# An attention, Fourier-mixing and feed-forward kernel: every engine in a hand-timed order, value sums by accumulating DMAs, and a two-round start of the feed-forward part

## The chip, the cores and the metric

The kernel runs on one core of a Trainium2 chip. The core has five engines that take instructions in order from queues of their own and meet through semaphores: PE (matmul, with its weight loads shown apart as PEld), DVE (vector), ACT (scalar and activation), POOL (GpSimd) and SP (only issues DMAs here). [...] The metric is the device time of one execution in microseconds; of several runs the median is taken.

## The reference

Inputs are q, k, v of shape (8 batches, 8 heads, 576 positions, 64) and two weights w_ch1 (512 x 2048) and w_ch2 (2048 x 512), which arrive as float64. Attention is computed twice and added: on means over four neighbouring positions (repeated back), and in a band of plus or minus three positions.

```python
q_d = q.reshape(B, H, Sd, 4, D).mean(axis=3)     # k_d and v_d alike
out_up = np.repeat(sm_attn(q_d, k_d, v_d), 4, axis=2)
mask = np.abs(pos[:, None] - pos[None, :]) < 4
...
x = out_up + np.matmul(softmax(where(mask, scores, -1e9)), v)
# moe part, x as (batch, 576, 512)
mixed = np.real(fft(fft(x, axis=1), axis=2))
u = x + mixed
un = (u - mean(u)) / np.sqrt(var(u) + 1e-06)
out = u + np.maximum(un @ w_ch1, 0.0) @ w_ch2
```

## The kernel before

The work falls into a front (attention and Fourier mixing, batch by batch) and a feed-forward part.

Local attention goes in 40 units, five to a batch; a unit holds two windows of 64 positions for all heads. A unit loads a slice of q and k (tile qkT) and of v (vaug), adds fours of columns of qkT for the pooled attention (`sum_in`), multiplies scores (tile sc), takes maxima, exponentials (sb), transposes (tpl, pT) and multiplies by v (av); DVE divides and writes to the x tiles of the batch, xa and xb.

Pooled attention goes in four steps of two heads for a batch (sp, sd, tp, ptd, avd). Its values are sums of four rows of v: `sum_v` loads a tile raw by SP (L213) and POOL adds twice (L214, L215) into the tile vsum. The result odt is stored to a DRAM buffer ud by SP (L292, `store`), repeated four times on the way, and `add_up` (L451) has four DMAs issued by POOL that add ud onto xa and xb.

Mixing (`Mix`) then works with xs = xa + xb on DVE (L458) and xm = xa - xb on POOL (L459), folds them over channels (xeo, then again into xa), splits the folded values into a rounded part fh and a remainder fl (`split`, fl on POOL at L494), and multiplies by cosine matrices over the sequence (tile y, `sequence`, nine matmuls for each of four parts) and over the channels (tile mix). `unfold` forms the sum oa and the difference xm on POOL (L558), which SP stores to a DRAM buffer um.

The feed-forward part works on 36 tiles of 128 rows. Blocks of 5, 4, ..., 4, 3 tiles go through 16 chunks of 128 hidden columns. A chunk of a block, called an item here, is twelve matmuls into hps (`first`, L730: high and low weight parts times high and low inputs), a ReLU on ACT into hh, the remainder hl on DVE (L734), and three matmuls a tile into the accumulators acc (`second`, L746 to L748). Tiles are prepared for the next block beside it: load from um, statistics, `norm`, transposition (tpn).

The weights arrive as 64 quarters of 256 columns, as float64 words. `to_f32` joins the two words of each to float32 on DVE (L123, L126, L131), with an absolute value on ACT (L130) and a guard that zeroes tiny values, on POOL (L135, L136) or DVE (L138) by a pattern. `part_weights` writes the rounded part by ACT and the remainder by POOL (L161).

What sets the order: PE's queue holds the order in which the code calls matmuls (a hand-written loop over steps, with `Stream` objects that put in pieces of folding and mixing at due times). The queues of the other engines are filled by a scheduler from priorities and a simulated timeline. Feed-forward work starts when the loop over steps is done; with two of 16 weight chunks decoded ahead, the rest are decoded while block 0 runs.

```python
main = unit_step(s) if s < NU + LAG else [lambda: None] * 4
...
fold_stream.run(4 * s + i + 1)
product_stream.run(4 * s + i + 1)
```

Of the kernel before, what the change touches and what calls it, by code (L numbers as in the profile page):

```python
# [41 lines left out]
CHUNKS = (1, 3, 4)

AHEAD = 2
NUM_PLACES = 4

GUARDS = "cc-c-"
WARM_UP = 12

TINY_HIGH = 1.125 * 2.0**-15  # L50


@with_exitstack
def kernel(
# [29 lines left out]
    NBLK = len(SIZES)  # L84
# [23 lines left out]
    places = [(res.tile([P, DM], F32, name="raw0"), res.tile([P, HN], I32, name="wt0"))]  # L108
# [8 lines left out]
    turns = [0]  # L117

    def to_f32(words, t):

        lo, hi = words[:, :, 0], words[:, :, 1]
        turns[0] += 1
        nc.vector.tensor_scalar(  # L123
            out=t, in0=hi, scalar1=3, scalar2=0x3FFFFFFF, op0=ALU.logical_shift_left, op1=ALU.bitwise_and
        )
        nc.vector.scalar_tensor_tensor(  # L126
            out=t, in0=lo, scalar=29, in1=t, op0=ALU.logical_shift_right, op1=ALU.bitwise_or
        )
        m, x = lo.bitcast(F32), t.bitcast(F32)
        nc.scalar.activation(out=m, in_=hi.bitcast(F32), func=AF.Abs)  # L130
        nc.vector.scalar_tensor_tensor(  # L131
            out=t, in0=hi, scalar=-0x40000000, in1=t, op0=ALU.bitwise_and, op1=ALU.bitwise_or
        )
        if GUARDS[turns[0] % len(GUARDS)] == "c":
            nc.gpsimd.tensor_scalar(out=m, in0=m, scalar1=TINY_HIGH, scalar2=None, op0=ALU.is_ge)  # L135
            nc.gpsimd.tensor_mul(out=x, in0=m, in1=x)  # L136
        else:
            nc.vector.scalar_tensor_tensor(out=x, in0=m, scalar=TINY_HIGH, in1=x, op0=ALU.is_ge, op1=ALU.mult)  # L138
        return x

    def fetch(raw, tm, f, w, j):

        src = wq[w - 1, f, j]
        if wide:
            nc.sync.dma_start(out=raw.bitcast(I32), in_=src.bitcast(I32))
            raw = raw.bitcast(I32).rearrange("p (n two) -> p n two", two=2)
        else:
            raw = raw[:, 0:HN]
            nc.sync.dma_start(out=raw, in_=src)
        return to_f32(raw, tm) if wide else raw  # L150

    def part_weights(f, w, j, raw, tm):

        x = fetch(raw, tm, f, w, j)
        if w == 1:
            x = x.rearrange("p (c f) -> p c f", c=2)
            h, l = (t[:, 2 * j : 2 * j + 2, :] for t in wts[f, 1])
        else:
            h, l = (t[:, j * HN : (j + 1) * HN] for t in wts[f, 2])
        nc.scalar.copy(out=h, in_=x)  # L160
        nc.gpsimd.tensor_sub(out=l, in0=x, in1=h.bitcast(F32))  # L161

    HD = DM // 2
    TB = BLK // P

    plocal, p1, pmix, pxs = (ExitStack() for _ in range(4))
    pf = pmix.enter_context(tc.tile_pool(name="pf", bufs=1, side="right"))
    p2 = plocal.enter_context(tc.tile_pool(name="p2", bufs=2))
# [5 lines left out]
    px = pxs.enter_context(tc.tile_pool(name="px", bufs=1, side="right"))  # L174
    vsum = [pd.tile([GH, 2, H, D + 1], F32, name=f"vsum{i}") for i in range(2)]
    for t in vsum:
        nc.gpsimd.memset(t, 1.0)
    zeros = pd.tile([8, DM], F32, name="zeros")
# [4 lines left out]

    def bank(name, rows=P):
        return banks.tile([P, DM], F32, name=name, tag="ps")[:rows]

    last, before = (B - 1) % NUM_X, (B - 3) % NUM_X

    xab = [None] * NUM_X
    for i in ((last + 1 + k) % NUM_X for k in range(NUM_X)):  # L190
        pool = pf if i == last else res if i == before else px
        xab[i] = [pool.tile([P, NSL, DM], F32, name=f"x{i}{j}") for j in "ab"]
# [3 lines left out]
    def zero_rows(b):  # L196

        for lo, hi in ((HS + 1, NUD + 1), (NUD + HS + 1, 2 * NUD)):
            nc.sync.dma_start(out=ud[b][lo:hi, :], in_=zeros[: hi - lo])
# [4 lines left out]
    class Pooled:  # L204
        def __init__(self, b):
            self.b, self.vs = b, vsum[b % 2]
            self.sd, self.pts = {}, {}

        def sum_v(self, i):

            h0, t = 4 * (i // 2), i % 2
            raw = pd.tile([GH, 4, 4 * D], F32, name="raw", bufs=NUM_RAW)
            nc.sync.dma_start(out=raw.rearrange("g r c -> g (r c)"), in_=vg[self.b, i])  # L213
            nc.gpsimd.tensor_add(out=raw[:, 0:2], in0=raw[:, 0:2], in1=raw[:, 2:4])  # L214
            nc.gpsimd.tensor_add(  # L215
                out=self.vs[:, t, h0 : h0 + 4, 0:D],
                in0=raw[:, 0].rearrange("g (h d) -> g h d", d=D),
                in1=raw[:, 1].rearrange("g (h d) -> g h d", d=D),
            )

        def scores(self, h0):
            qT, kT = sums[self.b]
            sd = self.sd[h0] = pd.tile([GH, 4, G], F32, name="sd", bufs=1)
            sps = [bank("sp", GH)[:, : 2 * G].rearrange("p (a g) -> p a g", a=2) for _ in range(2)]
            for t in range(2):
                for hl, sp in enumerate(sps):
                    r = slice(hl * D, hl * D + D)
                    nc.tensor.matmul(
                        sp[:, t, :],
                        qT[r, h0 // 2, t * GH : (t + 1) * GH],  # L230
                        kT[r, h0 // 2, :],
                        start=True,
                        stop=True,
                    )
            for hl, sp in enumerate(sps):
                mx = pd.tile([GH, 2], F32, name="mxd", bufs=4)
                nc.vector.tensor_reduce(out=mx, in_=sp, axis=AX.X, op=ALU.max)
                nc.vector.tensor_scalar_mul(out=mx, in0=mx, scalar1=-(2.0**-7))
                for t in range(2):
                    nc.scalar.activation(  # L240
                        out=sd[:, 2 * hl + t, :],
                        in_=sp[:, t, :],
                        func=AF.Exp,
                        scale=2.0**-7,
                        bias=mx[:, t : t + 1],
                    )

        def transpose_p(self, h0):
            self.pts[h0] = []
            for hl in range(2):  # L250
                tp = bank("tp", GH)[:, : 2 * G].rearrange("p (a g) -> p a g", a=2)
                for kt in range(2):
                    for t in range(2):
# [4 lines left out]
                        )  # L258
# [754 lines left out]
```

## Time and profile before

| | us |
|---|---|
| runs | 1397.17, 2261.53, 1392.53 |
| median | 1397.17 |
| the profiled execution | 1391.41 |
| its span, first to last instruction | 1389.6 |

Busy times in the span: PE 1214.0 us, DVE 636.9, POOL 369.0, ACT 292.3. In the prediction's rows a window is written start:end in us from the span's start; PEclk is the granted share of TensorE's clock, and the DMA share is the mean busy share of the core's 16 DMA engines. In a group's row stand the line, the engine, the operation, output<-inputs, shapes, count, busy us, mean ns of one, and the idle time before them with what ended it.

The 40 slices of the page below are 34.7 us each; digits are tenths of the slice.

```profile
PE   6774687759568966988999999999999999999998
DVE  5765485847657678789711311313113122131111
POOL 5424243534533467788400000000000000000000
PEclk8585769678687678999999999999999999999999
```

The first fifteen slices are the front, slices 16 to 20 the joint with feed-forward block 0 and the decoding, and the rest is feed-forward alone.

### The profile page before, as it was taken

The page shows a single profiled execution, that of the slowest core. Times are in us where ns is not written, and L with a number is a line of the kernel's source. Part 1 is how long each engine was busy: PE and PEld are TensorE (multiplying, and loading weights), DVE is VectorE, ACT ScalarE, POOL GpSimd, SP SyncE. Part 2 cuts the span into 40 slices and gives each one's busy share as a digit, 9 for nine tenths or more (in the row PEclk, how much of TensorE's full clock was granted, in tenths as well). Part 3 has the DMA queues.
Part 4 walks back from the last instruction along what each step waited for, and adds up shares of the span by engine and source line. Part 5 has one row for each costly group of instructions (what it writes and reads, how often), then busy time and mean ns, then how long its engine had stood idle before and what let it go on. Part 6 is the DMA issues. An engine that isn't in the chain of part 4 may idle for free.

```text
span 1389.6 us, 20511 instructions
## 1 busy us (share of the span) xinstructions
PE 1214.0 (87%) x8236; PEld 998.6 (72%) x8236; DVE 636.9 (46%) x1428; ACT 292.3 (21%) x678; POOL 369.0 (27%) x388
## 2 busy tenths in 40 slices
PE   6774687759568966988999999999999999999998
PEld 4663565548457755877788888888888888888897
DVE  5765485847657678789711311313113122131111
ACT  2331222223223221344311111111111111111110
POOL 5424243534533467788400000000000000000000
PEclk8585769678687678999999999999999999999999
DMA  7754627355562543343200100101001010010000
GB/s 234 238 174 111 158 86 179 109 140 171 133 152 70 152 116 84 119 129 123 91 0 0 61 1 0 61 0 61 1 0 61 0 53 9 0 53 0 1 31 23
DMA packets 50496, 110.84 MB, mean 80 GB/s; under 512 B 5494, under 2 KB 5784, under 8 KB 50144
## 3 DMA queue, kind: packets, MB, share of 16 engines
q1 hardware_dynamic: 44128, 95.82, 22.4%
q0 software_dynamic: 6272, 13.70, 5.1%
q8 instruction: 65, 1.06, 0.3%
q14 instruction: 31, 0.25, 0.1%
HBM read 81.20 MB, written 28.46 MB: 79 GB/s over the span
## 4 chain that ended last, share of the span: by engine, by line
PE 64%; DMA 15%; DVE 11%; POOL 5%; issue 4%; ACT 1%; SPq 0%; DVEq 0%; POOLq 0%; ACTq 0%
PE hps L730 25%; PE acc L748 9%; PE acc L747 9%; PE acc L746 8%; DMA ud<-odt 4%; DMA qkT<-in_qk_dram 3%; DMA x1b<-ud 3%; PE mix L534 2%; PE y L507 2%; PE avd L270 2%; PE sc L346 2%; DMA x2b<-ud 2%; DMA x0b<-ud 2%; DVE wt L126 1%; DVE xeo L467 1%
## 5 line engine op out<-in xcount | busy, mean ns | idle before, releaser
L730 PE MATMUL hps<-unT,w1h 128*128 128x512 f32 (+2 forms) x1280 | 322.6, 374 | 20.6 <-DVE hl L734 10.8
L734 DVE SCALAR_TENSOR_TENSOR hl<-hps,hh 128x512 fp32r<-128x512 f32 (+2 forms) x160 | 101.6, 635 | 446.7 <-ACT hh L733 446.6
L730 PEld LDWEIGHTS hps<-unT,w1h 128*128 128x128 f32 x1280 | 234.1, 191 | 62.6 <-DVE hl L734 11.2
L748 PE MATMUL acc<-w2h,hl 128*128 128x512 f32 x576 | 229.5, 398 | 5.8 <-DVE hl L734 5.4
L746 PE MATMUL acc<-w2h,hh 128*128 128x512 f32 x576 | 230.5, 400 | 4.6 <-ACT hh L733 4.6
L747 PE MATMUL acc<-w2l,hh 128*128 128x512 f32 x576 | 229.1, 398 | 0.0
L733 ACT ACTIVATE hh<-hps 128x512 fp32r<-128x512 f32 (+2 forms) x160 | 88.8, 555 | 598.5 <-PE hps L730 598.5
L683 POOL TENSOR_TENSOR rstd<-rstd,mhalf 128x1 f32<-128x1 f32 x36 | 20.2, 607 | 555.2 <-DVE rstd L682 553.3
L730 PE MATMUL hps<-unT,w1l 128*128 128x512 f32 (+2 forms) x640 | 160.2, 372 | 0.2 <-POOL w1l L161 0.2
L748 PEld LDWEIGHTS acc<-w2h,hl 128*128 128x128 f32 x576 | 109.2, 190 | 35.1 <-DVE hl L734 9.5
L730 PEld LDWEIGHTS hps<-unT,w1l 128*128 128x128 f32 x640 | 116.5, 190 | 20.0 <-POOL w1l L161 0.5
L746 PEld LDWEIGHTS acc<-w2h,hh 128*128 128x128 f32 x576 | 109.0, 189 | 28.3 <-ACT hh L733 5.4
L747 PEld LDWEIGHTS acc<-w2l,hh 128*128 128x128 f32 x576 | 109.2, 190 | 23.0
L400 PE MATMUL av<-vaug,pT 64*64 64x65 f32 x1280 | 57.9, 248 | 18.8 <-DVE odt L282 4.9
L270 PE MATMUL avd<-vsum,ptd 72*72 72x65 f32 x512 | 49.9, 263 | 25.2 <-ACT pT L383 17.6
L534 PE MATMUL mix<-chanm,yh 128*128 128x256 f32 (+1 forms) x192 | 48.1, 343 | 26.3 <-ACT sd L240 26.1
L400 PEld LDWEIGHTS av<-vaug,pT 64*64 64x64 f32 x1280 | 50.5, 159 | 26.6 <-issue 13.5
L346 PEld LDWEIGHTS sc<-qkT 64*64 64x64 f32 x1280 | 51.4, 165 | 22.4 <-issue 21.5
L270 PEld LDWEIGHTS avd<-vsum,ptd 72*72 72x72 f32 x512 | 45.1, 176 | 28.5 <-ACT pT L383 17.8
L507 PE MATMUL y<-seqm,fh 128*128 128x320 f32 (+1 forms) x192 | 57.9, 389 | 2.0 <-DVE xm L543 1.5
L346 PE MATMUL sc<-qkT 64*64 64x64 f32 x1280 | 57.5, 254 | 0.0
L534 PEld LDWEIGHTS mix<-chanm,yh 128*128 128x128 f32 (+1 forms) x192 | 32.0, 205 | 33.9 <-ACT sd L240 26.8
(151 smaller groups left out, 1578.3 us busy)
## 6 DMA issues: line engine op xcount, KB each, us to landing
qkT<-in_qk_dram SPq DMA_DIRECT2D x40, 512.0 KB
raw<-in_wq_dram SPq DMA_DIRECT2D x49, 256.0 KB
vaug<-in_vw_dram SPq DMA_DIRECT2D x40, 260.0 KB
raw<-in_vg_dram SPq DMA_DIRECT2D x32, 288.0 KB
ud<-odt SPq DMA_DIRECT2D x16, 576.0 KB
out_dram<-ut SPq DMA_DIRECT2D x16, 256.0 KB
x2b<-in_wq_dram SPq DMA_DIRECT2D x15, 256.0 KB
x2a<-um SPq DMA_DIRECT2D x15, 256.0 KB
```

Source lines behind the costliest of these rows:

```text
L270: nc.tensor.matmul(av[:, t, hl, :], self.pts[h0][hl][:, kt, t * GH : (t + 1) * GH], self.vs[:, kt, h0 + hl, :], start=(kt == 0), stop=(kt ...
L346: nc.tensor.matmul(sc[r, a * W : (a + 1) * W], self.qkT[r, 0, a // 2, o : o + W], self.qkT[r, 1, a // 2, o : o + W], start=False, stop=Tru ...
L400: nc.tensor.matmul(av[r, a, :], pT[r, 4 * hh + a], va[r, 4 * hh + a, :], start=True, stop=True)
L507: nc.tensor.matmul(y, l, r, start=(i == 0), stop=(i == len(mms) - 1))
L534: nc.tensor.matmul(ps[:, par * HD : (par + 1) * HD], l, r, start=(i == 0), stop=(i == len(mms) - 1), skip_group_check=True,)
L683: nc.gpsimd.tensor_tensor(out=rstd, in0=rstd, in1=mhalf, op=ALU.pow)
L730: nc.tensor.matmul(hps, a[:, c, :], unT[:, x, c, cols], start=(i == 0), stop=(i == len(mms) - 1))
L733: nc.scalar.activation(out=hh, in_=hps, func=AF.Relu)
L734: nc.vector.scalar_tensor_tensor(out=hl, in0=hps, scalar=0.0, in1=hh.bitcast(F32), op0=ALU.max, op1=ALU.subtract)
L746: nc.tensor.matmul(acc, hh[:, sl], w2h, start=(f == 0), stop=False)
L747: nc.tensor.matmul(acc, hh[:, sl], w2l, start=False, stop=False)
L748: nc.tensor.matmul(acc, hl[:, sl], w2h, start=False, stop=(f == NF - 1))
```

## The change

Everything is now put in program order on all engines. Each class has a `plan` that adds pieces of work to a list with a time, and the kernel runs the list sorted by time under `manual_schedule()` for all engines. The times only set the order, alike on every queue; a plan unit has no fixed length. A batch has 20 plan units, and the feed-forward part starts at unit 172. Functions are cut so that the part of each engine is an entry of its own.

```diff
+PACE = 20
+POOLED_AT = {0: 2, 1: 0, 2: -2}
+POOLED_LATER = -4
+MIX_AT = {0: 34, 1: 31}
+MIX_LATER = 28.5
+FFN_AT = 172
+ITEM = 1.45
+CHUNKS = (3, 6, 10, 16)
+ROUND = 6
+TILES = 4
...
+    def at(t, fn, *args):
+        events.append((t, len(events), partial(fn, *args)))
...
-        def sum_v(self, i):
-            h0, t = 4 * (i // 2), i % 2
-            raw = pd.tile([GH, 4, 4 * D], F32, name="raw", bufs=NUM_RAW)
-            nc.sync.dma_start(out=raw.rearrange("g r c -> g (r c)"), in_=vg[self.b, i])
-            nc.gpsimd.tensor_add(out=raw[:, 0:2], in0=raw[:, 0:2], in1=raw[:, 2:4])
...
+        def sum_v(self, r):
+            if r == 0:
+                self.vs = pd.tile([GH, 2, H, D + 1], F32, name="vsum", bufs=2)
+            eng = nc.gpsimd if r else nc.sync
+            how = {"accum_op": ALU.add} if r else {}
+            eng.dma_start(out=self.vs.rearrange("g t h d -> g (t h d)"), in_=vg[self.b, r], **how)
...
     class Pooled:
...
+        def plan(self):
+            b = self.b
+            for r in range(4):
+                at(pooled_at(b) - 8 + 2 * r, self.sum_v, r)
+            for i in range(H // 2):
+                t, h0 = pooled_at(b) + 5 * i, 2 * i
+                at(t, self.scores, h0)
...
+            at(t + 11.5, self.store)
...
     class Unit:
...
+        def plan(self):
+            t = 4 * self.u
+            at(pooled_at(self.b) - 14 + 2.6 * self.m, self.load)
+            at(pooled_at(self.b) - 2.8 + 0.5 * self.m, self.sum_in)
+            at(t, self.scores)
...
+            at(t + 10.9, self.result)
...
     class Mix:
...
+        def plan(self):
+            t = PACE * self.b + MIX_AT.get(self.b, MIX_LATER)
+            at(t, self.add_up)
+            at(t + 5.5, self.halves)
...
+            at(t + 11, self.split_low, 0)
...
+            at(u + 4.5, self.store)
...
     class Block:
...
+        def plan(self, t, f0, f1):
+            for f in range(f0, f1):
+                at(t, self.first, f)
+                at(t + 0.95 * ITEM, self.high, f)
+                at(t + 1.0 * ITEM, self.low, f)
+                at(t + 3 * ITEM, self.second, f, f == f0, f == f1 - 1)
+                t += 2 * ITEM
...
+    for n, f0, f1 in [(0, 0, ROUND), (1, 0, ROUND), (0, ROUND, NF)] + [(n, ROUND * (n == 1), NF) for n in range(1, NBLK)]:
+        starts[n] = t
+        t = blocks[n].plan(t, f0, f1)
...
+        if x.f < CHUNKS[0]:
+            decode(n, 50 + 9 * n, 8)
+        else:
+            begin = [t_a, t_e, t_d][sum(x.f >= c for c in CHUNKS[1:3])]
+            t = max(t + DECODE, begin + 0.3)
+            decode(n, t, 2)
...
+    with tc.manual_schedule():
+        for _, _, fn in sorted(events, key=lambda e: e[:2]):
+            fn()
```

Beside the order, the work itself changes in these places. The value sums are a plain load of the first quarter and three DMAs from POOL that add the others onto vsum; the host lays v out for this, with a column of 0.25 that sums to the ones column. The pooled maxima are scaled on ACT instead of DVE. `sum_in` adds q and k in one instruction, and one reciprocal serves both halves of a unit. In the decoding POOL clamps the absolute value between two limits (one instruction, `clamp`) in place of the guard's two, and DVE joins sign, exponent and fraction in three instructions (`join`); the fourth, L138, is gone. Twelve quarters (three chunks) are decoded during the front and the other 52 after the attention's last unit. xm, fl and the unfolding are POOL's in all batches. There are nine blocks of four tiles; block 0 and then block 1 first go through six chunks each, block 0 goes through the other ten, then block 1, and the partial results are added to u in between.

POOL's queue around the fold of batch 2, before: four x DMAs (xNa and xNb are the x tiles of a batch), then value additions, xm, and more value additions.

```order
L451 DMA x2a<-ud_59 64x2x512
L451 DMA x2b<-ud_59 64x3x512
L451 DMA x2a<-ud_59 64x3x512
L451 DMA x2b<-ud_59 64x2x512
L214 TENSOR_TENSOR raw<-raw 72x512 x2
L459 TENSOR_TENSOR xm<-x2a,x2b 128x1536
L380 MEMSET pT 64x8
L215 TENSOR_TENSOR vsum_106<-raw 72x4x64 x2
```

And with the change, the same place one batch later, where the order is the settled one:

```order
L494 DMA x1a<-ud_60 64x3x512
L494 DMA x1a<-ud_60 64x2x512
L494 DMA x1b<-ud_60 64x3x512
L494 DMA x1b<-ud_60 64x2x512
L167 TENSOR_TENSOR w1l_81<-wt_93,w1h_80 128x256
L225 DMA vsum<-in_vg_dram 72x1040 x2
L409 MEMSET pT 64x8
L502 TENSOR_TENSOR xm<-x1a,x1b 128x1536
L225 DMA vsum<-in_vg_dram 72x1040
L619 TENSOR_TENSOR oa<-xs,xm 128x512
L619 TENSOR_TENSOR xm<-xs,xm 128x512
```

Two of the three sum rounds of a later batch now stand between the fold's DMAs and xm, the third between xm and the unfolding of the batch before; each waits for the round ahead of it.

PE's queue where batch 7's sequence products (y, fh, fl) stand, before: all of them ahead of the first feed-forward product of block 0.

```order
L507 MATMUL y<-seqm,fh 128x320 x2
L507 MATMUL y<-seqm,fl 128x320
L730 MATMUL hps<-unT_5199,w1h_76 128x384 x4
L730 MATMUL hps<-unT_5199,w1l_77 128x384 x4
L730 MATMUL hps<-unT_5199,w1h_76 128x384 x4
```

With the change, after four items of block 0's first round (unT_5108 is block 0's input):

```order
L764 MATMUL acc<-w2h_86,hl 128x512
L571 MATMUL yz<-seqm,z 2x320 x6
L555 MATMUL y<-seqm,fh 128x320 x6
L555 MATMUL y<-seqm,fl 128x320 x3
L715 MATMUL tpn<-ident,un 128x128 x4
L744 MATMUL hps<-unT_5108,w1h_5206 128x512 x4
```

The last batch's products moved behind the first items of the feed-forward part, and each block item behind them in the queue comes after them.

More of the change, by code (lines that the diff above doesn't have):

```diff
@@ L115 @@
     wide = wq.dtype != F32
[L117 to L139, printed above, removed]
@@ L173 @@
     pd = p1.enter_context(tc.tile_pool(name="pd", bufs=1, side="right"))
[L174 to L178, printed above, removed]
+    zeros = pd.tile([8, D], F32, name="zeros")
     nc.gpsimd.memset(zeros, 0.0)
@@ L182 @@
     banks = pbank.enter_context(tc.tile_pool(name="banks", bufs=8, space=PSUM))
+    pools = {"banks": banks}
     def bank(name, rows=P):
[L185 to L192, printed above, removed]
+        return pools["banks"].tile([P, DM], F32, name=name, tag="ps")[:rows]
+    xab = [[px[i].tile([P, NSL, DM], F32, name=f"x{i}{j}") for j in "ab"] for i in range(NUM_X)]
     for t in (t for ts in xab for t in ts):
@@ L433, in __init__ @@
         def __init__(self, b):
-            self.b = b
-        def engines(self, names):
-            on = ON_POOL[min(self.b, len(ON_POOL) - 1)]
-            return [nc.gpsimd if n in on else nc.vector for n in names]
+            self.b, self.y = b, {}
         def add_up(self):
@@ new lines, with close_b @@
+    blocks = [Block(n) for n in range(NBLK)]
+    pacc = [None]
+    for b in range(B):
+        pooleds[b].plan()
+        mixes[b].plan()
+    for u in units:
+        u.plan()
+    at(10, constants)
+    at(36, clear_yz)
+    t_b = PACE * (B - 1) + POOLED_LATER + 15 + 11.6
+    t_a = 4 * (NU - 1) + 11
+    t_c = PACE * (B - 1) + MIX_LATER + 13.6
+    t_e = PACE * (B - 1) + MIX_LATER + 20.9
+    t_d = PACE * (B - 1) + MIX_LATER + 22.5 + 7.5 + 4.6
+    def close_b():
+        p1.close()
+        early = pool("early")
+        uts[0] = [early.tile([P, DM], F32, name=f"ut0{i}") for i in range(TILES)]
+        unTs[0] = early.tile([P, 2, NCC, TILES * P], F32R, name="unT0")
@@ new lines, with decode @@
+    t = FFN_AT
+    starts = {}
+    for n, f0, f1 in [(0, 0, ROUND), (1, 0, ROUND), (0, ROUND, NF)] + [(n, ROUND * (n == 1), NF) for n in range(1, NBLK)]:
+        starts[n] = t
+        t = blocks[n].plan(t, f0, f1)
+        if f1 == NF and 0 < n < NBLK - 1:
+            for i in range(TILES):
+                at(starts[n] + 6 + 0.5 * i, blocks[n + 1].load, i)
+                v = starts[n] + 12 + i * (t - starts[n] - 18) / TILES
+                blocks[n + 1].prepare(i, v, v + 1)
+    def decode(n, t, ahead):
+        x = quarters[n]
+        at(t - ahead, x.fetch)
+        at(t, x.size)
+        at(t + 0.5, x.clamp)
+        at(t + 1.2, x.join)
+        at(t + 2.1, x.high)
+        at(t + 2.5, x.low)
```

697 lines of the change are left out of this document (306 added, 391 removed).

## The prediction

> **What bounds the kernel now.** I read the chain of waits first (which stretch ends how), then busy times by stretch, then the groups of one engine. In the chain, "x..<-ud" marks the accumulating DMAs that add the pooled attention of one batch to its local attention, and "hps" the first feed-forward product. Columns: start, duration, what.
>
> ```profile
> 93.73 7.83 DMA ud<-odt
> 103.37 10.94 DMA x0b<-ud
> ...
> 160.50 10.82 DMA x1b<-ud
> ...
> 225.59 14.28 DMA x2b<-ud
> ...
> 288.42 10.52 DMA x0b<-ud
> ...
> 349.97 14.58 DMA x1b<-ud
> ...
> 405.03 9.42 DMA x2b<-ud
> ...
> 515.01 11.35 DMA x1b<-ud
> ...
> 532.32 2.93 PE hps L730 x12
> ...
> 693.46 2.79 PE hps L730 x12
> ...
> 1316.10 2.09 PE hps L730 x12
> ```
>
> Batch 1's DMA stands at 160.50 and batch 7's at 515.01: six batches in 354.5 us, 59.1 us each. From 532 the first feed-forward block (5 tiles) runs beside the rest of the front, and from 693 to 1316 seven blocks of 4 tiles run alone. Busy times of three stretches (length, then busy us and count of each engine, granted clock, DMA share, GB/s):
>
> ```profile
> core 0: us, PE busy (x) PEld busy (x) DVE busy (x) ACT busy (x) POOL busy (x), PEclk, DMA share, GB/s
> 160.50:515.01 354.51, 255.86 (x2877) 209.19 (x2873) 235.28 (x604) 97.08 (x251) 159.97 (x145) 0.76 0.50 130
> 515.01:693.46 178.45, 155.51 (x797) 132.87 (x798) 145.42 (x271) 60.64 (x157) 129.92 (x138) 0.92 0.38 114
> 693.46:1316.10 622.64, 622.64 (x2749) 506.27 (x2749) 140.49 (x263) 80.36 (x137) 14.43 (x26) 1.00 0.06 20
> ```
>
> Three regimes. The front (row 1): per batch PE is busy 42.6 us, DVE 39.2, POOL 26.7, DMA engines 29.5 (0.50 of 59.1), so nothing is full and the 59.1 us are waits; the granted clock is only 0.76. The joint (row 2): 178 us, DVE and POOL at 81% and 73%, since the weights are decoded there. The pure feed-forward (row 3): PE 100% at clock 1.00, 622.64/7 = 88.95 us for a block. Only the first two can change; 36 tiles cost 9 x 88.95 = 800.6 us in either kernel.
>
> **What a front batch costs PE at full clock.** Between 200 and 230 us PE was never idle and the clock 1.00:
>
> ```profile
> 200.00:230.00 30.00, 30.00 (x438) 25.05 (x435) 23.54 (x66) 12.48 (x34) 14.12 (x14) 1.00 0.69 192
> PE 1214.0 (87%) x8236; PEld 998.6 (72%) x8236; DVE 636.9 (46%) x1428; ACT 292.3 (21%) x678; POOL 369.0 (27%) x388
> L730 PE MATMUL hps<-unT,w1h 128*128 128x512 f32 (+2 forms) x1280 | 322.6, 374 | 20.6 <-DVE hl L734 10.8
> L730 PE MATMUL hps<-unT,w1l 128*128 128x512 f32 (+2 forms) x640 | 160.2, 372 | 0.2 <-POOL w1l L161 0.2
> L746 PE MATMUL acc<-w2h,hh 128*128 128x512 f32 x576 | 230.5, 400 | 4.6 <-ACT hh L733 4.6
> ```
>
> The first row is the engines' busy time in that stretch, the second the page's totals. 8236 matmuls less 1920 first, 3 x 576 second, 144 transposes of normed tiles and 12 warm-up ones leave 4432, 554 a batch; at 30.00/438 us each that is 38 us. The change removes none of them. So the new front cannot run under about 38 us a batch.
>
> **DVE.** From 39.2 a batch: the scaling of the pooled maxima (row L238 below, 17.7/8 = 2.2) goes to ACT, which is busy 16 us of 59; the merged reciprocals and window sums save about 1; the 12 weight quarters now decoded early add 1.5 a batch at the three join rows, 0.49 + 0.67 + 0.61 = 1.8 each, though some decoding is in the 39.2 already. I take 38. The fourth join step, L138 (in 26 of 64 quarters), goes.
>
> ```profile
> L238 DVE TENSOR_SCALAR mxd<-mxd 72x2 f32<-72x2 f32 x64 | 17.7, 297 | 0.0
> L123 DVE TENSOR_SCALAR wt<-raw 128x256 int32<-128x256 int32 x49 | 24.0, 490 | 18.5 <-DMA raw<-in_wq_dram 13.6 <-POOL w1l L161 4.8
> L126 DVE SCALAR_TENSOR_TENSOR wt<-raw,wt 128x256 int32<-128x256 int32 x49 | 32.6, 669 | 0.5
> L131 DVE SCALAR_TENSOR_TENSOR wt<-raw,wt 128x256 int32<-128x256 int32 x49 | 29.7, 611 | 0.3
> ```
>
> **POOL, where I expect the front to be bound.** The value sums leave it as arithmetic (L214 and L215: (44.2 + 25.2)/8 = 8.7 us a batch) and come back as three accumulating DMAs, each of which waits, at the head of POOL's queue, for the one before. Behind the first wait stand xm, the three unfolds and the two fl splits, on which DVE and then PE wait. (The row with 160.50:515.01 is POOL's time in the x issues of L451 alone; the two rows of xNN<-ud end with the median us to landing.)
>
> ```profile
> L214 POOL TENSOR_TENSOR raw<-raw 72x512 f32<-72x512 f32 x32 | 44.2, 1382 | 45.3 <-DMA raw<-in_vg_dram 44.6 <-PE tp L254 0.6
> L215 POOL TENSOR_TENSOR vsum<-raw 72x256 f32<-72x256 f32 x32 | 25.2, 801 | 21.1 <-PE avd L270 20.7
> L558 POOL TENSOR_TENSOR oa<-xs,xm 128x512 f32<-128x512 f32 x24 | 32.2, 1343 | 47.4 <-DVE xm L543 21.5 <-DVE mxd L238 12.8 <-DVE rs L404 12.4
> L459 POOL TENSOR_TENSOR xm<-x1a,x1b 128x1536 f32<-128x1536 f32 x3 | 13.3, 4424 | 19.6 <-DMA x1b<-ud 16.1 <-DVE wt L123 3.6
> L494 POOL TENSOR_TENSOR fl<-x2a,fh 128x512 fp32r<-128x512 f32 x6 | 7.6, 1278 | 19.4 <-ACT fh L492 19.3
> L135 POOL TENSOR_SCALAR raw<-raw 128x256 f32<-128x256 f32 x29 | 32.3, 1113 | 20.5 <-ACT raw L130 16.2 <-DVE mxd L238 4.3
> L161 POOL TENSOR_TENSOR w1l<-wt,w1h 128x256 fp32r<-128x256 f32 x32 | 27.6, 866 | 7.6 <-ACT w1h L160 7.5
> 160.50:515.01 354.51, 23.98 (x25) 0.76 0.50 130
> x0b<-ud POOLq DMA_DIRECT2D x3, 384.0 KB, 7.8
> x2a<-ud POOLq DMA_DIRECT2D x2, 384.0 KB, 10.9
> POOL x2a L451 <- DMA ud<-odt: 13.4, 2, 7.2
> ```
>
> Round POOL's loop of one batch, at 1.0 us an issue (23.98/25): four x issues 3.8; the first sum round is issued next, 1.0, and its data stand behind the x data, which land 11.8 us after the last x issue (mean of the six chain rows 160.50 to 515.01). How long an accumulating sum round of 300 KB takes, no row shows. Four x DMAs, 1280 KB, pass in those 11.8 us, 108 KB/us, so 300 KB need 2.8; the nearest single landings are 7.8 and 10.9, with four in flight. I take 3 behind the x data and 5 for a lone one. Round two is issued at 14.8 after the last x issue, xm (4.3) hides all but 0.7 of its 5, round three is issued at 21.8; then three unfolds 6 x 1.34 = 8.0, two fl of 768 columns 3 x 1.28 = 3.8, one and a half clamps and lows (1.11 + 0.87) 3.0, memsets 0.3. Sum 40.7. Waiting for the ud store before the fold is 0 to 7.2 in the last row; the new order leaves six plan units between store and fold, so I take 2.6. **Period 43.3 us.** Ends: nothing for the rounds and the store gives 37, under PE's 38; 10.9 for each round and 7.2 gives 59.
>
> [...]
>
> **The joint.** PE's time in the y matmuls of one batch (36 of them) and in 31 mix matmuls, both at clock 1.00:
>
> ```profile
> 200.00:230.00 30.00, 6.99 (x36) 5.30 (x36) 1.00 0.69 192
> 320.00:340.00 20.00, 5.20 (x31) 3.53 (x29) 1.00 0.59 184
> ```
>
> 52 of 64 quarters are decoded after the attention ends. POOL: 52 x 1.98 = 103 us plus batch 7's fold and unfold and batch 6's unfold, some 30 more. DVE: 52 x 1.77 = 92; the 22 items and eight prepared tiles, some 1.7 blocks at 140.49/7 = 20 us, 34; batch 7's fold and mixing, which I put at two fifths of a batch's 38, 16: together about 142. PE has, until block 0 ends, 22 items of 88.95/16 = 5.6 us, and the mixing of batch 7 (y 7.0 for its 36 matmuls, mix 6.0 at 5.20/31, yz 1) and of 6's rest (6), 142 us. The round order (6 of 16 chunks for block 0, then for block 1) gives the decoding 12 items of cover instead of the two chunks ahead of before. If that cover is late, PE waits at its head: batch 7's sequence products stand between hps groups. Before, the joint lost 178.45 less 5/4 x 88.95 = 111 and two batches' mixing (28), some 40 us. DVE and PE now have 142 us each; batch 7's fold takes a dozen us from the fold's DMA to fl while DVE is already full, so I take 15; ends 0 and 40.
>
> **The start.** Until the first fold some 14.3 MB (ten qk tiles, nine v tiles, constants, the first sums and stores) must move; the page's first two slices moved 234 and 238 GB/s:
>
> ```profile
> GB/s 234 238 174 111 158 86 179 109 140 171 133 152 70 152 116 84 119 129 123 91 0 0 61 1 0 61 0 61 1 0 61 0 53 9 0 53 0 1 31 23
> 1384.12 0.24 PE acc L748
> ```
>
> 14.3/0.236 = 61, so the fold of batch 0 starts at 60 instead of 103.
>
> **Sum.** Fold of batch 0 at 60; seven periods, 7 x 43.3 = 303; the 3.5 plan units to the first feed-forward item, 7.6: it starts at 371 (532 before). Then 800.6, mixing of batch 7 and the rest of 6 on PE 20, the joint's loss 15, and the end 5.2 (1384.36 to 1389.6). Span 1211.5; the profiled execution took 1391.41 for a span of 1389.6, so 1213. That execution lies 0.4% under the median of the runs, 1397.17. Per period P: time = 910 + 7 P.
>
> **Rivals.**
> *PE becomes the bound*, P 38 to 40: 1176 to 1190. For it: DVE and PE both need 38. Against: three queues in strict order, each 90% full, must never wait for long, and a long wait is paid again in clock:
>
> ```profile
> 240.00:260.00 20.00, 11.97 (x108) 9.73 (x110) 20.00 (x42) 5.06 (x11) 14.53 (x12) 0.54 0.32 97
> ```
>
> after the fold's wait near 240 PE's granted clock was 0.54, against 1.00 at 200 to 230. [...]
> *The sum rounds are as slow as the x DMAs*, P 50 to 59: 1260 to 1323. For it: the DMA engines go from 29.5 busy us in 59 to some 35 in 43 (three rounds at 2.8, less the plain reads).
> *The order does not shorten the front*: P stays 59.1, 1324, 5% faster and only through start and joint.
> *POOL's queue runs serially* (the other side): 26.4 us of work, x data at the worst row 14.58, three rounds at 10.9 each in nobody's shade: 73.7 a batch, 1426, slower. It decides only from P = 73.7 upward; xm between rounds two and three speaks against it. From 65.7 (1369) the result is no change.
>
> **Numbers.** Forecast P 40 to 50, 1190 to 1260: 0.52. PE-bound 0.13. Slow rounds 0.18. Front as before up to the 2% line 0.05. Serial POOL 0.12, of it 0.05 within 2% and 0.07 beyond. So faster 0.88, same 0.05, slower 0.07; 2% is about what a measurement of this kernel can tell. The range 1165 to 1320 holds the first three and little else.
>
> **What would show it.** Right: x..<-ud DMAs 41 to 46 us apart; POOL waiting longest at the second vsum issue on the first; clock near 1.00 in the front; first hps near 371; blocks still 89 us. Wrong: POOL idle little while DVE waits for qkT or xs for longer than 5 us a batch (the bound is elsewhere), a joint with over 40 us of PE idle, or a period over 50.

## The result, and the profile after

| | before | changed |
|---|---|---|
| median, us | 1397.17 (3 runs) | 1335.49 (4 runs) |
| ratio, 95% interval | | 0.9565 [0.950, 0.963] |
| profiled execution, its span, us | 1391.41, 1389.6 | 1341.46, 1339.7 |

One run of before (2261.53 us) and one of e11 below (1329.25 us) were slow outliers, and the medians and ratios here leave them out. The change makes the kernel 4.4% faster, not 13%. The forecast of 1213 us is 122 us too low, and its range ends at 1320.

The timeline of the changed kernel shows where the forecast parts from the run. Columns: start, duration, engine, line, operation, tiles, and in brackets the idle time before it and what ended it. The x..<-ud rows are the first fold DMAs of batches 0, 1, 6 and 7.

```profile
82.49 0.82 POOL L225 DMA_DIRECT2D vsum<-in_vg_dram  x1 [32.05 <-PE tp L262]
...
83.40 2.04 POOL L494 DMA_DIRECT2D x0a<-ud  x2
...
127.58 2.39 POOL L494 DMA_DIRECT2D x1a<-ud  x2
...
421.66 2.06 POOL L494 DMA_DIRECT2D x0a<-ud  x2 [7.13 <-DMA ud<-odt]
...
482.71 2.28 POOL L494 DMA_DIRECT2D x1a<-ud  x2
...
492.66 1.91 PE L744 MATMUL hps<-unT,w1h 128*128 128x512 f32 x4
```

The first fold starts at 83.4 instead of 60. Seven periods take 399.3 us, 57.0 each instead of 43.3; before, a period was 59.1. The first feed-forward product starts at 492.7 instead of 371. From there to the end it is 847.0 us, against 841 by the forecast's terms. So of the 128 us that this execution's span lies above the forecast, nearly all lie in the front: 23 us of start and 96 us of period. In the kernel before, the same seven periods (from the first fold DMA of batch 0 to that of batch 7) went from 98.90 to 510.22, 411.3 us or 58.8 each. Of the 50 us that the span lost, they gave only 12; the start gave 16 and what lies behind the folds 22.

Busy times by stretch (length, then busy us and count of each engine, granted clock, DMA share, GB/s):

```profile
83.40:482.71 399.31, 320.83 (x3551) 247.85 (x3551) 278.08 (x611) 124.42 (x320) 162.76 (x151) 0.78 0.59 148
492.66:640.00 147.34, 138.02 (x598) 108.99 (x598) 120.27 (x215) 49.59 (x122) 87.08 (x111) 0.93 0.34 99
640.00:1240.00 600.00, 600.00 (x2683) 493.90 (x2682) 154.97 (x286) 81.58 (x141) 19.98 (x35) 1.00 0.07 25
```

In a period of the front PE is now busy 45.8 us and idle 11.2, DVE is busy 39.7 and idle 17.3, POOL is busy 23.3. The granted clock is 0.78, about that of before. Some of the idle times between first and last fold, those of POOL, PE and DVE that matter here: engine and line, what was waited for, us in total, times, longest:

```profile
POOL vsum L225 <- DMA vsum<-in_vg_dram: 87.3, 11, 15.1
...
PE sp L236 <- DVE sums L359: 38.1, 6, 8.4
...
DVE mx L381 <- PE sc L369: 24.4, 14, 5.0
DVE yl L564 <- ACT yh L561: 20.7, 13, 3.1
DVE wt L146 <- POOL wt L138: 15.0, 3, 9.4
...
DVE xs L501 <- DMA x0b<-ud: 0.4, 1, 0.4
```

The fold's transfers are off DVE's queue, as the new order meant: xs waits 0.4 us in all. What came in their place is waiting between PE and DVE in both directions, and POOL's wait for the sum rounds. A stretch of batch 4 on the timeline:

```profile
308.64 0.49 DVE L564 TENSOR_TENSOR yl<-y,yh 128x320 fp32r<-128x320 f32 x1 [2.84 <-ACT yh L561]
314.14 0.69 DVE L381 TENSOR_REDUCE mx<-sc 128x8 f32<-128x512 f32 x1 [5.01 <-PE sc L369]
...
322.13 1.21 DVE L359 TENSOR_REDUCE sums<-qkT 128x256 f32<-128x1024 f32 x1
323.26 0.68 DVE L604 SCALAR_TENSOR_TENSOR xm<-xm,mix 128x512 f32<-128x512 f32 x1
323.85 1.08 DVE L359 TENSOR_REDUCE sums<-qkT 128x224 f32<-128x896 f32 x1
324.85 3.15 DVE L501 TENSOR_TENSOR xs<-x0a,x0b 128x1536 f32<-128x1536 f32 x1
327.93 1.17 DVE L359 TENSOR_REDUCE sums<-qkT 128x96 f32<-128x384 f32 x2
329.01 0.28 DVE L146 TENSOR_SCALAR wt<-wt 128x256 int32<-128x256 int32 x1
...
333.88 1.04 DVE L359 TENSOR_REDUCE sums<-qkT 128x216 f32<-128x864 f32 x1
334.98 1.24 PE L236 MATMUL sp<-sums 64*72 64x144 f32 x8 [8.14 <-DVE sums L359]
```

Until 312 PE runs sequence products and then the next scores, and DVE has little to do: it waits for these scores, 5.0 us. From 322 to 335 DVE has everything at once: the five reductions `sum_in`, xs of the fold, a join of weights and results of mixing. PE needs the last of the five reductions for sp and stands still for 8.1 us. Neither engine is full over the period; each is the late one for a part of it.

### The profile page after: what moved, and what is told of

Same layout as the page of the kernel before. It is cut to its first block, busy times and chain, and to the rows that moved or that the text cites. A ratio compares the mean times of both kernels' runs of the same rounds, so it can differ in the third digit from the quotient of the medians.

```text
span 1339.7 us, 19636 instructions
## 1 busy us (share of the span) xinstructions
PE 1219.7 (91%) x8070; PEld 984.0 (73%) x8072; DVE 619.5 (46%) x1250; ACT 296.2 (22%) x678; POOL 289.3 (22%) x330
## 4 chain that ended last, share of the span: by engine, by line
PE 71%; DVE 14%; DMA 7%; issue 3%; POOL 2%; SPq 2%; ACT 0%; DVEq 0%; POOLq 0%
PE hps L744 27%; PE acc L762 9%; PE acc L763 9%; PE acc L764 9%; PE y L555 4%; DMA vsum<-in_vg_dram 3%; PE sc L369 2%; PE av L421 2%; DVE sums L359 2%; DVE wt L149 1%; PE avd L281 1%; DMA ud<-odt 1%; PE mix L592 1%; PE sp L236 1%; PE tpn L715 1%
## 5 line engine op out<-in xcount | busy, mean ns | idle before, releaser
L744 PE MATMUL hps<-unT,w1h 128*128 128x512 f32 x1152 | 313.7, 394 | 1.7 <-DVE xs L604 1.7
L752 DVE SCALAR_TENSOR_TENSOR hl<-hps,hh 128x512 fp32r<-128x512 f32 x144 | 99.3, 690 | 451.5 <-ACT hh L748 451.5
L744 PEld LDWEIGHTS hps<-unT,w1h 128*128 128x128 f32 x1152 | 215.9, 189 | 47.4 <-DVE xs L604 1.9
L748 ACT ACTIVATE hh<-hps 128x512 fp32r<-128x512 f32 x144 | 86.0, 597 | 499.9 <-PE hps L744 499.8
L744 PE MATMUL hps<-unT,w1l 128*128 128x512 f32 x576 | 156.4, 394 | 0.0
L744 PEld LDWEIGHTS hps<-unT,w1l 128*128 128x128 f32 x576 | 109.1, 189 | 24.1
L236 PE MATMUL sp<-sums 64*72 64x144 f32 x256 | 31.2, 378 | 48.3 <-DVE sums L359 48.3
L236 PEld LDWEIGHTS sp<-sums 64*72 64x72 f32 x256 | 20.2, 183 | 52.8 <-issue 27.5
L724 DVE TENSOR_TENSOR unT<-tpn,unT 128x512 fp32r<-128x512 f32 x36 | 24.6, 688 | 72.1 <-ACT unT L721 72.1
L225 POOL DMA_DIRECT2D vsum<-in_vg_dram x24 | 21.0, 873 | 165.5 <-DMA vsum<-in_vg_dram 122.4
```

Of the source, the lines that this page charges most:

```text
L236: nc.tensor.matmul(sp[:, t, :], qT, s[r, 1, h0 // 2, :], start=True, stop=True)
L724: nc.vector.tensor_sub(out=self.turned(i, 1), in0=self.tp[i].rearrange("p (c n) -> p c n", c=NCC), in1=self.turned(i, 0).bitcast(F32),)
L744: nc.tensor.matmul(hps, a[:, c, :], unT[:, x, c, :], start=(i == 0), stop=(i == len(mms) - 1))
L748: nc.scalar.activation(out=hh, in_=self.hps[f], func=AF.Relu)
L752: nc.vector.scalar_tensor_tensor(out=hl, in0=self.hps[f], scalar=0.0, in1=self.hh[f].bitcast(F32), op0=ALU.max, op1=ALU.subtract)
```

## The experiments

"Front" below is the time from the first fold DMA of batch 0 to that of batch 7, and "PE clock" the granted clock in it, both from each run's profile. That is one execution of the run and can lie 10 us or so from its median (e6: 1323.3 against 1335.9), so differences of a few us between two fronts mean little. A period is the front over 7.

### Three suspects: the rounds, the clock, both

First theory: POOL, waiting for the sum rounds at the head of its queue, holds the front. Rival: PE at half its clock does. Run e1 moved the rounds of later batches ahead of the fold's DMAs, e2 put twelve filler matmuls ahead of the sequence products, e3 left rounds 1 to 3 out, and e4 is e1 with e2.

```diff
# e1
+t0, t1 = pooled_at(b - 2) + 25.2, PACE * (b - 2) + MIX_AT.get(b - 2, MIX_LATER) - 0.3   # b > 1
-at(pooled_at(b) - 8 + 2 * r, self.sum_v, r)
+at(t0 + (t1 - t0) * r / 3, self.sum_v, r)
# e2
+at(t + 13.95, self.keep, 12)    # 12 x matmul(w, identb, maskb), batches 0 to 6
# e3
-for r in range(4):
-    at(pooled_at(b) - 8 + 2 * r, self.sum_v, r)
+at(pooled_at(b) - 8, self.sum_v, 0)
```

> The four sum rounds of a batch move ahead of the fold's four x DMAs in POOL's queue (from batch 2 on), into the stretch where POOL has nothing else to do; the work is the same. The changed kernel runs in 1335 us with 57.0 us between folds. Theory Q (POOL's waits for the rounds, behind which xm, the unfolding and the clamps stand, hold the front): the period falls to 46 to 50, the time to 1260 to 1295. Theory C (the front is held by PE at half its clock, whatever makes it idle first): the period stays above 53, the time between 1310 and 1345.

> Twelve dummy matmuls of 512 columns stand in PE's queue just ahead of each batch's sequence products (batches 0 to 6), on tiles that are there anyway; their result is not used. [...] Theory C: the sequence products, which ran at a granted clock of 0.50 in three or four batches, run at 1.00; some 75 us of PE work at half clock is halved, less 7 times 2.6 to 5.1 for the dummies: 1305 to 1325 us. Theory Q: the dummies only add, 1335 to 1365 us.

> The three accumulating rounds are left out: vsum holds the first quarter of v's rows alone, so the pooled values are not the reference's; all else is done. Theory Q: the period falls to 44 to 48, the time to 1245 to 1280, a little under the run with the rounds moved. Theory C: 1300 to 1340.

> The rounds moved and the dummies put in. Theory Q: as with the rounds moved alone or up to 25 us slower, 1260 to 1320. Theory C: 1290 to 1320, faster than either alone. If both hold, each for its part, 1240 to 1280.

| run | median us | ratio, 95% | first fold | front | PE clock |
|---|---|---|---|---|---|
| changed | 1335.5 | 0.957 [0.950, 0.963] | 83.4 | 399.3 | 0.78 |
| e1 | 1346.4 | 0.963 [0.959, 0.967] | 84.4 | 404.3 | 0.80 |
| e2 | 1329.5 | 0.953 [0.948, 0.957] | 77.2 | 395.1 | 0.85 |
| e3 | 1312.2 | 0.941 [0.935, 0.947] | 71.1 | 376.5 | 0.83 |
| e4 | 1351.0 | 0.968 [0.964, 0.971] | 84.1 | 410.2 | 0.83 |

Without any rounds the front is still 53.8 us a batch, so the first theory does not hold; rounds ahead of the fold (e1) do not help either. Neither theory forecast the whole set: e3 lies in the rival's range, e1 just above it, e2 between the two, and e4 above every range that was named. What e3 does show is a part of the start: without the rounds the first fold stands at 71 and not at 83. The row at 82.49 above says why: the first accumulating round of batch 2, in POOL's queue ahead of that fold, waited at the head of the queue for 32 us until then. The fillers are no clean test, since they cost PE time of their own; the group of e2 in its front (last columns: busy us, mean ns of one, idle time before):

```profile
L638 PE MATMUL warm<-maskb,identb 128*128 128x512 bf16 x77 | 24.8, 468 | 0.9 <-issue 0.7
```

PE's busy time fell from 320.8 to 311.3 us with these 24.8 in it, so its other work took 34 us less at the higher clock (0.85 against 0.78). The front got 4 us shorter.

### Which engine's work is on the path

Second theory, from the stretch shown above: DVE and PE take turns in the listed order. Run e5 is e2 with e3. Run e6 spreads the reductions a little in batches 4 to 7, e7 lists the mixing of batches 2 to 6 later, and e8 leaves out the decoding of the 12 early quarters.

```diff
# e6, b > 3
-at(pooled_at(self.b) - 2.8 + 0.5 * self.m, self.sum_in)
+at(pooled_at(self.b) - 4.9 + 0.95 * self.m, self.sum_in)
# e7
-MIX_AT = {0: 34, 1: 31}
+MIX_AT = {0: 34, 1: 31, 2: 33, 3: 33, 4: 33, 5: 33, 6: 33}
# e8, x.f < CHUNKS[0]
-decode(n, 50 + 9 * n, 8)
+at(50 + 9 * n + 2.1, x.blank)      # ACT writes zeros to both parts
```

> Both of two earlier edits at once: rounds 1 to 3 of the value sums are left out (the pooled half then sums only the first quarter of the values), and 12 filler matmuls stand ahead of each of the first seven sequence products. Alone the first gave 1312 us and the second 1329 us against 1335 us for the changed kernel. If the clock and POOL's waits are two separate delays on one chain, the gains add: 1300 to 1308 us. If each hides behind the other (whoever is last sets the fold), the pair gives more than the sum: 1250 to 1290 us. If neither is the limit and VectorE and TensorE work in turns in the listed order, the pair gives no more than the first alone: 1308 to 1320 us.

> Nothing is left out; for batches 4 to 7 the five reductions of q and k over groups of four stand 2.1 to 0.3 list units earlier and are spread over 3.8 list units instead of 2, so that fewer of them stand in one block with the fold of the batch before. If VectorE and TensorE work in turns because the list puts the reductions and the fold in one stretch of VectorE (about 30 us in which TensorE waits for sums): 3 to 6 us less in each of four batches, 1310 to 1325 us. If the clock or POOL's waits for the value sums set the period: 1330 to 1342 us.

> Nothing is left out; the mixing of batches 2 to 6, from the fold to the store, stands 4.5 list units later against the two attentions, so that the fold's VectorE work no longer meets the reductions of q and k, and the sequence products meet other units. If the turns of VectorE and TensorE set the period: 3 to 8 us less a batch over five batches, 1295 to 1320 us. If the clock or POOL's waits set it: 1328 to 1345 us, as the changed kernel or a little more, because each fold is listed later.

> The decoding of the first 12 quarters of the weights, which the list puts into the front, is left out: the first three of the 16 slices of the feed-forward use weights of zero, written by ScalarE. This takes 12 clamps from POOL's queue, where some of the 15 us waits for ScalarE stand, and 36 instructions of 0.4 to 3.2 us from VectorE. If POOL's order holds the front (a clamp behind a round's wait, and VectorE's join behind the clamp): 4 to 7 us less a batch, 1285 to 1310 us. If turns of VectorE and TensorE hold it: about 3 us less a batch, the joins' own time, 1310 to 1322 us. If the clock holds it: 1325 to 1340 us.

Then one engine's work was made less where it stands (e9, e10), and the decoding was moved, alone (e11) and with e7 (e12).

```diff
# e9, batches 0 to 6
-mms += [(fl[:n, t, T, :], seqm[:n, 0, T // 2, t, :]) for t, n in slots]
# e10
-nc.vector.tensor_reduce(out=to, in_=x[:, :, a - g0 : e - g0], axis=AX.X, op=ALU.add)
+nc.vector.tensor_reduce(out=to, in_=x[:, :, a - g0 : e - g0, :1], axis=AX.X, op=ALU.add)
# e11
-decode(n, 50 + 9 * n, 8)
+b = n // 2
+decode(n, PACE * b + MIX_AT.get(b, MIX_LATER) + 15.5 + 2.5 * (n % 2), 8)
```

> The three of nine matmuls of each sequence product that use the low part of the folded input are left out for batches 0 to 6 (the low parts are still made). They take 19.8 + 14.1 = 34 us of TensorE between the first and the last fold of the changed kernel. If TensorE and VectorE work in turns, each on the chain for a part of every batch, most of it comes off the time: 1300 to 1318 us. If VectorE's work and POOL's order alone set the period: 1328 to 1340 us. If TensorE at its granted clock is the one bound: all of it, 1298 to 1306 us.

> The sums of q and k over four neighbours are left out down to their first element (the pooled attention then takes one row of four), so that VectorE's reductions read a quarter of the elements: 34 us between the first and the last fold of the changed kernel become an estimated 8 to 14 us. If TensorE and VectorE work in turns: most of the 20 to 26 us comes off, 1308 to 1322 us. If TensorE at its granted clock is the one bound: 1328 to 1340 us. If VectorE is the one bound: all of it, 1305 to 1315 us.

> Nothing is left out; the 12 early quarters of the weights are decoded two to a batch at the list places where TensorE runs the sequence products and VectorE has little listed, instead of every 9 list units. Leaving them out gave 1310.5 us against 1335 us. If it was the place that cost (VectorE's 16 us of joins and 15 us of waits for POOL's clamps inside its own busy stretch): most of the 25 us comes back, 1310 to 1322 us. If the work costs the same wherever it stands: 1330 to 1340 us.

> Nothing is left out; the mixing of batches 2 to 6 stands 4.5 list units later (alone 1308 us) and the early quarters are decoded beside the sequence products. If both only shorten VectorE's stretch in which TensorE waits, the gains add to most of their sum: 1280 to 1298 us. If the move of the mixing already took the decoding out of that stretch, or POOL's waits for the value sums are next: 1300 to 1312 us.

| run | median us | ratio, 95% | first fold | front | PE clock |
|---|---|---|---|---|---|
| e5 fillers, no rounds | 1322.4 | 0.947 [0.943, 0.950] | 71.9 | 392.2 | 0.85 |
| e6 reductions spread | 1335.9 | 0.954 [0.949, 0.960] | 77.5 | 390.3 | 0.81 |
| e7 mixing later | 1308.4 | 0.937 [0.934, 0.939] | 81.9 | 365.6 | 0.82 |
| e8 no early decoding | 1310.5 | 0.939 [0.934, 0.943] | 77.0 | 376.3 | 0.80 |
| e9 less PE work | 1326.0 | 0.949 [0.944, 0.955] | 81.3 | 390.1 | 0.78 |
| e10 less DVE work | 1325.0 | 0.949 [0.943, 0.954] | 82.8 | 390.1 | 0.78 |
| e11 decoding moved | 1306.4 | 0.934 [0.927, 0.941] | 76.2 | 365.4 | 0.85 |
| e12 e7 and e11 | 1295.6 | 0.928 [0.923, 0.933] | 79.3 | 357.4 | 0.81 |

Two moves that leave nothing out, e7 and e11, give 27 and 29 us, and 40 together. Moving the decoding gave as much as leaving it out, so its place cost, not its work. Where the fillers and the missing rounds meet (e5) nothing adds up; the pair is no faster than e3 alone. Spreading the reductions by two list units (e6) did nothing that can be told from noise. The theory of turns had e7, e12 and, at the edge, e8 in its ranges, and e11 gained a little more than it said. It missed e6, which came out where the rival had it, and e5, e9 and e10 lie outside every range that was named.

PE's largest wait, for the sums of q and k, shows that e7 did what it was meant to do, since it was 38.1 us in the changed kernel. The first row is e7's, the second that of e9, where PE had less work:

```profile
PE sp L236 <- DVE sums L359: 20.0, 6, 5.8
```

```profile
PE sp L236 <- DVE sums L359: 45.6, 6, 13.4
```

The front rows of e9 and of e10:

```profile
81.27:471.37 390.10, 290.21 (x3476) 231.02 (x3475) 277.30 (x611) 124.36 (x323) 161.52 (x151) 0.78 0.61 152
```

```profile
82.75:472.87 390.12, 319.42 (x3560) 247.03 (x3559) 265.94 (x611) 125.38 (x323) 163.35 (x152) 0.78 0.61 152
```

e9 took 30.6 us off PE (320.83 to 290.21) and e10 12.1 us off DVE (278.08 to 265.94); the front got shorter by the same 9.2 us in both. The expectation for e10 was 20 to 26 us off DVE, so that edit was a smaller one than planned. In these single executions a microsecond of DVE was worth 0.76 and one of PE 0.30. With so small a gain (the intervals of both overlap that of the changed kernel) this is a hint and no measurement, though it goes against PE as the one bound: a part of what e9 took off PE came back as waiting for DVE's sums. How much of the time DVE's queue is on the path is not shown. What e11 changed in DVE's waits:

```profile
DVE mx L381 <- PE sc L369: 16.9, 11, 2.6
...
DVE yl L564 <- ACT yh L561: 9.8, 9, 3.1
...
DVE wt L146 <- POOL wt L138: 4.1, 3, 3.2
```

The waits for clamps fell by 11 us, as intended, and those for scores and for ACT's part of the products by another 18, which the edit did not touch. That fits a late DVE making PE late, and PE then DVE. The clock is a rival here: in e11 PE's busy time fell by 29.3 us with the same work (to 291.5, clock 0.85), its idle time by only 4.6. e9 took as much off PE and gained 9.5 us in the median where e11 gained 29, so the shorter PE time alone does not explain e11; what the clock's part was is open.

### The better order: what the clock and the rounds are worth in it

Runs e13 to e15 add the fillers, the missing rounds, and both, to e12. Run e16 lists the mixing later still.

```diff
# e16, against e12
-MIX_AT = {0: 34, 1: 31, 2: 33, 3: 33, 4: 33, 5: 33, 6: 33}
+MIX_AT = {0: 34, 1: 35, 2: 36, 3: 36, 4: 36, 5: 36, 6: 34}
```

> Nothing is left out; the kernel with the mixing 4.5 list units later and the decoding beside the sequence products (1296 us), with 12 filler matmuls ahead of each of the first seven sequence products. If the low granted clock in the products is a delay that the old order covered: 1270 to 1288 us. If it lies beside VectorE's stretch anyway, and the fillers cost what they bring: 1288 to 1302 us.

> The same better order (1296 us), with rounds 1 to 3 of the value sums left out, so that the pooled half sums only the first quarter of the values. If POOL's waits for the rounds are a delay of their own: 23 us less as in the old order, 1265 to 1280 us. If the later mixing already took the fold's transfers out from behind them: 1285 to 1298 us.

> The better order (1296 us) with the fillers and with rounds 1 to 3 of the value sums left out (only the first quarter of the values is summed). If three separate delays make up the difference between 57 and 43 us a batch, all are gone now: 1225 to 1262 us. If the waits between the engines in the listed order remain whatever the clock and the rounds do: 1268 to 1295 us.

> Nothing is left out; the better order (1296 us) with the mixing another 3 list units later for batches 2 to 5, 4 for batch 1, and 1 for batch 6. If the gain of the first move came from parting the fold from the reductions, which 4.5 units have done: 1290 to 1305 us, a little more for later folds. If the fold still meets work that it should not: 1278 to 1290 us.

The last two runs take up the largest waits of DVE (for clamps) and of PE (for sums) in e16: e17 joins the early quarters 2.5 list units later, behind the clamp, and e18 also spreads the reductions as e6 did.

```diff
# e17, against e16, early quarters
-at(t + 1.2, x.join)
+at(t + 3.7, x.join)
```

> Nothing is left out; the kernel with the mixing 7.5 list units later (1286 us), in which VectorE joins each early quarter 3.2 instead of 0.7 list units behind POOL's clamp. VectorE waited 23 us for clamps there. If a wait at the head of VectorE's queue costs the path its length: 1266 to 1276 us. If the work behind it has slack: 1281 to 1290 us.

> The same, and the five reductions of batches 4 to 7 spread over 3.8 list units and begun 2.1 units earlier, where TensorE now runs the sequence products. TensorE waited 27 us for reductions, about half of it in these batches. In the old order the same edit gave nothing (1336 us against 1335 us). If the reductions now hold TensorE: another 8 to 14 us, 1254 to 1268 us. If TensorE's waits have slack: as the run with the later join, within 5 us.

| run | median us | ratio, 95% | first fold | front | PE clock |
|---|---|---|---|---|---|
| e13 e12, fillers | 1301.1 | 0.931 [0.927, 0.935] | 83.8 | 368.3 | 0.84 |
| e14 e12, no rounds | 1291.6 | 0.924 [0.921, 0.927] | 71.5 | 363.0 | 0.81 |
| e15 e12, both | 1292.6 | 0.924 [0.922, 0.926] | 72.5 | 362.0 | 0.87 |
| e16 mixing later still | 1285.7 | 0.920 [0.917, 0.923] | 80.3 | 343.6 | 0.85 |
| e17 e16, join later | 1282.2 | 0.921 [0.917, 0.925] | 76.4 | 337.2 | 0.87 |
| e18 e17, reductions spread | 1284.7 | 0.922 [0.919, 0.925] | 79.8 | 343.3 | 0.83 |

In the better order neither the rounds nor the fillers gain beyond the intervals. So the 23 us of e3 are no fixed price of the rounds; what they cost depends on the order. All six runs lie in a range that was named: e13 to e15, e17 and e18 in that of waits with slack, e16 in that of a fold that still met other work. The front of e16, and some of its waits between first and last fold:

```profile
80.25:423.82 343.57, 290.20 (x3532) 228.04 (x3529) 270.58 (x607) 123.09 (x318) 170.08 (x151) 0.85 0.69 173
```

```profile
PE sp L236 <- DVE sums L359: 27.2, 6, 6.0
...
DVE wt L146 <- POOL wt L138: 21.0, 5, 6.1
DVE mx L381 <- PE sc L369: 11.2, 9, 2.6
```

DVE's work a batch is nearly unchanged (38.7 us against 39.7), its idle time fell from 17.3 to 10.4 us a batch, PE's from 11.2 to 7.6. PE's busy time fell by 30.6 us with nearly the same count of matmuls (3532 and 3551), as the clock rose from 0.78 to 0.85 without a filler. So of the 55.7 us that the front lost, 30.6 were PE's busy time and 25.1 its idle time; how much of the gain is due to the waits and how much to the clock, these runs do not tell apart. e17 took the clamps' wait off DVE's list of waits, but its ratio is within the interval of e16: those 21 us were slack there. In their place DVE's xs waited for the fold's transfers again, 16.2 us:

```profile
DVE xs L501 <- DMA x0b<-ud: 8.8, 3, 5.3
...
DVE xs L501 <- DMA x1b<-ud: 7.4, 2, 5.0
```

Both e16 and e17 beat the changed kernel by some 50 us.

## Why the prediction was wrong

*What held.* The sign was right, and so was the feed-forward alone, with PE at 100% and clock 1.00. Everything from the first hps to the end took 847 us (841 forecast), so the terms for tiles, mixing, joint and tail have the right sum. DVE's 38 us of work a batch were 39.7, and the 5 us for a lone sum round were 4.5 at the median. The page's DMA row has that landing time as its last number, the size before it:

```profile
vsum<-in_vg_dram POOLq DMA_DIRECT2D x24, 292.5 KB, 4.5
```

The longest wait of POOL in the front is for sum rounds, as forecast.

*The step that failed* is the period: "Round POOL's loop of one batch ... Sum 40.7", and 43.3 with the store. It took the longest queue for the bound and let the other two engines run beside it at no cost. In its place the runs showed PE and DVE waiting for each other in the listed order: in 57.0 us PE was idle for 11.2 and DVE for 17.3. POOL's loop can be made shorter by all of its rounds (e3, 53.8 us a batch) and the period stays ten above the forecast. The rival "the sum rounds are as slow as the x DMAs" had the period in its range (50 to 59), but not for its reason: the rounds landed in 4.5 us at the median, and without any the period is 53.8. The rival "the order does not shorten the front" was the one that came true in the main: period 59.1 there, 57.0 here; 1324 us there, 1335 here, with start and joint as the only large gains. It got a chance of 0.05, and the prediction gives no reason for so little. DVE's largest waits of before were for the fold's transfers (xs waited 74.4 us for them in the front), and the list did remove these (0.4 us):

```profile
DVE xs L458 <- DMA x0b<-ud: 31.8, 3, 15.0
DVE xs L458 <- DMA x1b<-ud: 28.7, 2, 17.1
...
DVE xs L458 <- DMA x2b<-ud: 13.9, 2, 10.2
```

No row in the prediction shows the new waits between DVE and PE, but the list's times were there to read. Take them modulo 20, that is by their place inside a batch's 20 list units. The reductions of one batch (pooled_at - 2.8 to - 0.8, which is 13.2 to 15.2), xs of the batch two before (14.0) and its channel folds (15.5 to 20) stand in one third of the period on DVE, with pooled scores that need the reductions at 16 on PE; the sequence products stand at 3 to 8, where DVE has little.

*How much of it is shown.* With nothing left out, other list times alone take the front from 399 to 344 us (e16). That is 55 of the 96 us by which the seven periods were missed. That the order is the cause of these is shown; by which of its waits, and how much of it through the clock, is argued. The remaining 41 (49.1 against 43.3 a batch) are open: e17 and e18 took on the largest waits of DVE and PE and gained nothing that can be told from e16.

*The start*, "14.3/0.236 = 61", counted bytes alone. One part of the 23 us is the round that stands in POOL's queue ahead of the first fold: the four runs without rounds fold first at 71.1 to 72.5, all others at 76.2 to 84.4, so it costs some 4 to 13 us. The rest is a chain that the sum has no term for, the pooled attention of batch 0. In e3 DVE ends its result only at 62.42, SP then issues the stores to ud, and the fold, which reads ud, follows:

```profile
62.00 0.42 DVE L298 TENSOR_TENSOR odt<-avd,rsd 72x256 f32<-72x256 f32 x1
...
62.45 1.70 SPq L308 DMA_DIRECT2D ud<-odt  x2
...
64.20 1.85 SPq L312 DMA_DIRECT2D ud<-odt  x1
...
71.06 2.09 POOL L493 DMA_DIRECT2D x0a<-ud  x2 [4.09 <-DMA qkT<-in_qk_dram]
```

That the store's landing is what the fold waited for is read from this order and from the code; the bracket names another transfer.

*The clock*, forecast near 1.00, was 0.78. By itself it is not shown to cost much: 30.6 us less of PE's work brought 9 (e9), and the fillers' higher clock, 0.85, 4 us of front (e2). No run shows the 2.6 to 5.1 us for a dozen fillers that the sum for e2 counts; in e13 a dozen took 2.76 to 4.83 us, and in e2 77 of the 84 took 24.8. But the clock rose as the order got better, and most of what PE gained in e11 and e16 is busy time, so its part in those gains is open. The price of the low clock alone was not isolated, because fillers cost PE 25 us.

## What to carry to other kernels

When two in-order queues that feed each other are 70 and 80% full, as DVE and PE are here, the sum of one queue is a lower bound and no forecast: lay the list out modulo the period and look for places where one engine has everything and its partner nothing. Before you pay for a suspect (slow rounds, low clock), shift the phase of one stage by a fifth of the period; here that was worth as much as leaving out the rounds or the early decoding (27 us against 23 and 25), and what the suspects seemed to cost was within the intervals afterwards.

## What the runs showed of the hardware

*PE, busy, ran 20 us at a granted clock of 0.50.* In the changed kernel, PE was by the profile busy without a break and the granted clock 0.50:

```profile
290.00:300.00 10.00, 10.00 (x64) 7.51 (x64) 3.42 (x7) 2.50 (x6) 0.40 (x1) 0.50 0.77 214
300.00:310.00 10.00, 10.00 (x68) 7.66 (x66) 3.35 (x11) 2.59 (x9) 4.70 (x5) 0.50 0.93 233
```

The work was sequence products with small matmuls between them, and it ran 20 us at 0.50 in these two rows. Why it did so was not tested.

*DVE instructions took longer beside one of POOL's: 3.27 us against 0.28, 3.15 against 1.75.* In e2, POOL's xm and DVE's first join instruction ran at the same time, after xs had run ahead of xm:

```profile
312.29 1.75 DVE L501 TENSOR_TENSOR xs<-x0a,x0b 128x1536 f32<-128x1536 f32 x1
...
314.74 3.42 POOL L502 TENSOR_TENSOR xm<-x0a,x0b 128x1536 f32<-128x1536 f32 x1 [0.28 <-POOL pT L409]
...
315.04 3.27 DVE L146 TENSOR_SCALAR wt<-wt 128x256 int32<-128x256 int32 x1
```

The join takes 0.28 us in the median of the changed kernel's 64 (329.01 above is one) and took 3.27 here, ending 0.15 us behind xm. In the stretch of batch 4 above it is xs that ran beside xm, and it took 3.15 us instead of 1.75:

```profile
322.91 3.47 POOL L502 TENSOR_TENSOR xm<-x0a,x0b 128x1536 f32<-128x1536 f32 x1 [0.28 <-POOL pT L409]
```

Of the changed kernel's eight xs, the three with no arithmetic of POOL beside them (from 97.68, 199.20 and 251.50) took 1.75 to 1.76 us. The one from 146.52 took 3.85 beside an xm begun at 145.34, and the one from 501.40 took 2.84 beside an unfolding begun at 501.18. Where xs began first, at 388.11 and 444.38, it took 1.75, and POOL's instruction was the longer one: xm 4.49 instead of 3.42, the unfolding (oa) 2.74 against a median of 1.46. What set these times was not tested.
